# Windowed attention and two dense layers in float32: the first projections in five blocks of tokens (384, 512, 512, 512, 384) where there were six of 384, on one core

## The chip, the cores and the metric

The kernel runs on one core of one Trainium2 chip. The metric is the time of one execution in device microseconds (us), as a median of several runs. Profiles are of one execution each. TensorE (PE) multiplies matrices, VectorE (DVE), ScalarE (ACT) and GpSimd (POOL) work on tiles, SyncE (SP) issues loads.

## The reference

Everything is float32. Attention runs over 4 x 8 heads of 576 positions and 64 dimensions, and each position sees itself and the 63 before it. Its output, 2304 tokens of 512 numbers, goes through a gated product and two further layers:

```python
scores = scale * np.matmul(q, k.transpose(0, 1, 3, 2))
...
mask = (rel >= 0) & (rel < window)
scores = np.where(mask, scores, -1000000000.0)
...
attn = attn / (np.sum(attn, axis=-1, keepdims=True) + 1e-09)
return np.matmul(attn, v).astype(np.float32)
...
a = x @ w1
b = x @ w2
h = a * b @ w3
return (h @ w_out).astype(np.float32)
...
h = x @ w_in
g = h * (1.0 / (1.0 + np.exp(-h)))
return (g @ w_out).astype(np.float32)
```

w1 and w2 are 512 x 1024, w3 is 1024 x 1024, the first w_out 1024 x 512, w_in 512 x 2048 and the second w_out 2048 x 512.

## The kernel before, in words

**Stages.** The program has three stages, in this order.

1. `phase_w` multiplies w3 by the first w_out (matmul L482), so that the two layers become one matrix, `wp`. Weights arrive as 64-bit numbers and are converted on ACT, DVE and POOL. The first 14 groups of attention run between its matmuls.
2. `phase_a(blk, hooks)` is called once for each of six blocks of 384 tokens. It computes a = x w1, b = x w2, the product p = a b, and x2 = p wp, which goes to DRAM (`x2d`). Between its matmuls it runs the attention of the *next* block, and hooks of other work: in block 0 the rest of the conversions, in block 5 the conversion of the last two weights.
3. The last two layers run over blocks of 512 tokens (`emit_h`, L633, and `emit_o`, L652).

**Split operands.** A factor is held as a high part of reduced precision and the rest, and a product is three matmuls (`PASSES`). `split` makes the two parts: a copy on ACT (L79), a subtraction on POOL or DVE (L82).

**A block of `phase_a`.** It has 24 units. Units 0 to 15 are 12 matmuls each (L510) into one bank, `ab`, 8 pairs in turn: an even unit s gives a half of a, which ACT copies out (L516); the odd unit after it gives b, and DVE multiplies it by that copy (L518), after which ACT (L79) and POOL (L82) split the product into `p` or `q`. Units 16 to 23 are 12 matmuls each (L530), two units for each of four `x2` tiles, copied out by ACT (L535). So a block has 16 x 12 + 4 x 24 = 288 matmuls, each as wide as the block has tokens.

**A group of attention.** A group g is one unit of 128 tokens (`u`) and one pair of heads (`c`). There are 72, 12 for each block. A group is issued in two halves by `half(h)`, h = 2g and 2g + 1. The even half is: the scores of g on PE (L266, L270) and their mask and minimum on DVE (L276); the values of g-2 on PE (L343, L344); the transposes of g-1 on PE (L309), split by ACT (L319, L321) and DVE (L322, L324) into `pt`; the exponentials of g on ACT (L287). The odd half is: the sum's addition, the reciprocal and the product on DVE (L295, L297, L299), which finish `sm` of g; two copies on ACT (L349, L350), two additions on DVE (L351, L352) and one on POOL (L353), which put the values of g-2 into `xr`; the split of q and k of g+2 on ACT (L241), POOL (L245) and DVE (L248); the split of v of g. The first 17 groups (`plain`) are computed without split operands. They take other matmuls (L262, L336 to L338) and little on the other engines.

**What sets the order.** Every engine works through its instructions in the order in which the program issues them, and that order is written by hand: `unit(n)` issues one half in front of each unit (24 halves in 24 units), so that PE has one even half in front of every second unit. There is one bank for scores (`s`) and one for transposes (`t`). PE does the transposes of g-1 right after the scores of g, and they need `sm` of g-1 from DVE.

**Buffers.** Tiles of one tag share a buffer and wait for its last reader. Keys of plain groups (`k_p`) and the low part of keys of the others (`k_lo`) have buffers of their own, and so have the plain values `v_p` and the others.

Of the kernel before, what the change touches and what calls it, by code (L numbers as in the profile page):

```python
# [42 lines left out]
def tile_window_attention_ffn(ctx, tc, qkv, vp, mask, ident, w1, w2, w3t, w_out, w_in, w_out2, out):  # L43
# [158 lines left out]
    def plain(g):  # L202


        return g < PLAIN

    def place(g):
        blk, r = divmod(g, 3 * NPAIR)
        return blk * 3 + r % 3, r // 3

    def load_qk(g):
        if g < NG and g not in loaded:
            loaded.add(g)
            u, c = place(g)
# [4 lines left out]
            qk_raw[g] = att.tile([128, 128], F32, name=f"qp{g}", tag="qp", bufs=2)  # L219
            nc.sync.dma_start(out=qk_raw[g], in_=qkv[u, c, :, 0:128])  # L220

            for h, hs in HEADS:
                n = slice(384 + h * 192, 576 + h * 192)
                nc.sync.dma_start(out=k_p[g % 2][hs, h * 192 : h * 192 + 192], in_=qkv[u, c, hs, n])

    def load_v(g):
        if g < NG and ("v", g) not in loaded:
            loaded.add(("v", g))
            if plain(g):
                nc.sync.dma_start(out=v_p[g % 3], in_=vp[g])  # L230
                return
            v_raw[g] = att.tile([128, 3, 64], F32, name=f"v{g}", tag="v", bufs=3)
            u, c = place(g)
            nc.sync.dma_start(out=v_raw[g].rearrange("p t d -> p (t d)"), in_=qkv[u, c, :, 768:960])

    def prep_qk(g):
        if g >= NG or plain(g):
            return
        t = qk_raw.pop(g)
        hi = att.tile([128, 768], F32R, name=f"qkhi{g}", tag="qkhi", bufs=2)  # L240
        nc.scalar.copy(out=hi, in_=t)  # L241
        q, k = slice(128, 384), slice(384, 768)
        for h, hs in HEADS:
            n = slice(384 + h * 192, 576 + h * 192)
            nc.gpsimd.tensor_tensor(  # L245
                out=k_lo[g % 2][hs, h * 192 : h * 192 + 192], in0=t[hs, n], in1=f32(hi[hs, n]), op=ALU.subtract
            )
        nc.vector.tensor_tensor(out=hi[64:128, q], in0=t[64:128, q], in1=f32(hi[64:128, q]), op=ALU.subtract)  # L248
        qk_st[g] = hi

    def prep_v(g):
        if plain(g):
            return
        vhl = att.tile([128, 3, 2, 64], F32R, name=f"vhl{g}", tag="vhl", bufs=2)
        split(vhl[:, :, 0], vhl[:, :, 1], v_raw.pop(g), "act", "pool")
        v_st[g] = vhl

    def scores(g):
        s_ps = psa.tile([128, 2, 192], F32, name=f"s{g}", tag="s")
        t = qk_raw.pop(g) if plain(g) else qk_st.pop(g)  # L260
        if plain(g):
            nc.tensor.matmul(s_ps, lhsT=t[:, 0:128], rhs=k_p[g % 2], start=True, stop=True)  # L262
        else:
            for h in range(2):

                nc.tensor.matmul(  # L266
                    s_ps[:, h], lhsT=t[:, 128 + h * 128 : 256 + h * 128],
                    rhs=t[:, 384 + h * 192 : 576 + h * 192], start=(h == 0), stop=False,
                )
# [87 lines left out]
    def half(h):  # L357
# [4 lines left out]
        if not odd:  # L362
# [5 lines left out]
                split_t(g - 1, transposes(g - 1))  # L368
            if g < NG:
                exps(g)  # L370
            if g >= 2 and (g - 2) % (3 * NPAIR) == 3 * NPAIR - 1:
                sums.pop()()
        else:
            if g < NG:
# [21 lines left out]
            halves[0] += 1  # L396

    def split_x(blk, c):
        if c == 0:
            xhl[blk] = [slot(f"{t}{blk}", t, [2, 2, NB], F32R) for t in ("xa", "xb")]  # L400
        x = xhl[blk][c // 2][:, c % 2]
        split(x[:, 0], x[:, 1], xr[:, c], "act", "pool")


    W_HALVES = 28

    def phase_w():
        wo = slot("wo", "p", [8, 512])
        q = slot("q", "q", [2304])
# [80 lines left out]


    def phase_a(blk, hooks):
        x = xhl[blk]
        p = [slot(f"p{blk}", "p", [5, 2, NB], F32R), slot(f"q{blk}", "q", [3, 2, NB], F32R)]
        p = [p[f // 5][:, f % 5] for f in range(8)]
        a_sb = None

        def unit(n):
            halves_to(W_HALVES + 24 * blk + n + 1)
            hooks(n)  # L500

        for s in range(16):
            f, m = divmod(s, 2)
            unit(s)
            fs = slice((f % 4) * 128, (f % 4 + 1) * 128)
            acc = accumulator(f"ab{blk}_{s}", [128, NB])
            for k in range(4):
                w = weights["12", (2 * m + f // 4) * 4 + k]
                for n, (l, r) in enumerate(PASSES):
# [2 lines left out]
                        start=(k == 0 and n == 0), stop=(k == 3 and n == 2),  # L512
                    )
            if m == 0:
                a_sb = slot(f"a{blk}_{f}", "st", [2, NB], bufs=4)
                nc.scalar.copy(out=a_sb[:, 0], in_=acc)  # L516
            else:
                nc.vector.tensor_tensor(out=a_sb[:, 1], in0=acc, in1=a_sb[:, 0], op=ALU.mult)  # L518
                split(p[f][:, 0], p[f][:, 1], a_sb[:, 1], "act", "pool")
        for o in range(4):  # L520
            acc = accumulator(f"x2_{blk}_{o}", [128, NB])
            for f in range(8):
                if f % 4 == 0:
                    unit(16 + 2 * o + f // 4)
# [4 lines left out]
                for n, (l, r) in enumerate(PASSES):  # L529
# [178 lines left out]
def plain_values(qkv):  # L708
# [53 lines left out]
```

## Time and profile before

| | |
|---|---|
| median of 3 runs | 869.71 us (869.51 to 870.24) |
| the profiled execution | 868.85 us |
| its span, first to last instruction | 867.1 us |
| PE busy | 847.3 us (98%) |
| ACT busy | 497.8 us (57%) |
| DVE busy | 452.3 us (52%) |
| POOL busy | 445.6 us (51%) |
| `phase_w` | 9.6 to 97.6 us |
| block 0 of `phase_a` | 97.6 to 163.2 us |
| blocks 1 to 4, all with attention | 163.2 to 414.3 us |
| block 5 and the last two layers | from 414.3 us |

The shares of busy time are means over stages that differ: the engines other than PE do most of their work before 414.3 us. The profiled execution lies 0.86 us below the median and takes 1.75 us more than its span.

### The profile page before, as it was taken

Reading aid. Unit: us, or ns where it says so; the run is one execution under the profiler, and the core shown is the slowest. Engines: PE = TensorE matmul, PEld = TensorE weight load, DVE = VectorE, ACT = ScalarE, POOL = GpSimd, SP = SyncE. Lnnn points to the kernel's source line nnn. Section 1 sums busy time; section 2 is a strip of 40 time slices with the busy share of each in tenths; the row PEclk is TensorE's granted clock in tenths of the full one; section 3 lists DMA queues with packets and bytes.
Section 4 is the critical chain, followed back from the end, with each engine's and each line's share of the span. In section 5 each row is a group of like instructions: output and inputs, shape, how many; then the busy total and the mean of one; then the engine's idle time right before and its main releaser. Section 6 shows DMA issues by size and latency. Waiting matters only on the chain.

```text
span 867.1 us, 13353 instructions
## 1 busy us (share of the span) xinstructions
PE 847.3 (98%) x4362; PEld 737.0 (85%) x4362; DVE 452.3 (52%) x1158; ACT 497.8 (57%) x1243; POOL 445.6 (51%) x494
## 2 busy tenths in 40 slices
PE   5999999999999999999999999999999999999998
PEld 2444799999999999999998888888888888888896
DVE  5989878778778778676465884111111111111111
ACT  6888868788788788786666774222222222222222
POOL 4768566666666666665685886223322232223222
PEclk9999999999999999999999999999999999999999
DMA  8998233323333333330687200200020002000100
GB/s 296 336 291 261 95 97 108 120 92 101 120 92 110 112 95 120 118 92 33 245 319 274 82 1 0 98 1 1 0 98 1 1 0 73 2 1 0 49 1 25
DMA packets 43204, 85.83 MB, mean 99 GB/s; under 512 B 4864, under 2 KB 22528, under 8 KB 43136
## 3 DMA queue, kind: packets, MB, share of 16 engines
q1 hardware_dynamic: 37088, 75.55, 26.8%
q10 hardware_dynamic: 6048, 9.44, 3.0%
q8 instruction: 35, 0.57, 0.3%
q14 instruction: 33, 0.27, 0.1%
HBM read 75.53 MB, written 9.44 MB: 98 GB/s over the span
## 4 chain that ended last, share of the span: by engine, by line
PE 86%; DVE 1%; ACT 1%; issue 0%; POOLq 0%; POOL 0%; ACTq 0%; DVEq 0%
PE h L633 23%; PE o L652 23%; PE ab L510 22%; PE x L530 12%; PE t L309 2%; PE o L343 2%; PE s L266 1%; PE s L270 1%; PE o L344 1%; ACT sm L287 0%; DVE rs L295 0%; DVE a L518 0%; ACT p L79 0%; DVE cv_b L128 0%; POOLq L758 0%
## 5 line engine op out<-in xcount | busy, mean ns | idle before, releaser
L82 POOL TENSOR_TENSOR g<-sg,g 128x512 fp32r<-128x512 f32 (+1 forms) x80 | 94.9, 1186 | 249.6 <-ACT g L79 235.1
L633 PE MATMUL h<-x2t,hl 128*128 128x512 f32 (+1 forms) x960 | 213.4, 371 | 0.0
L652 PE MATMUL o<-hl,g 128*128 128x512 f32 x864 | 211.2, 391 | 0.1
L639 DVE TENSOR_TENSOR sg<-h,sg 128x512 f32<-128x512 f32 (+1 forms) x80 | 51.1, 638 | 288.2 <-ACT sg L638 288.2
L633 PEld LDWEIGHTS h<-x2t,hl 128*128 128x128 f32 x960 | 169.4, 188 | 33.9
L652 PEld LDWEIGHTS o<-hl,g 128*128 128x128 f32 x864 | 160.9, 188 | 35.6 <-POOL g L82 0.5
L638 ACT ACTIVATE sg<-h 128x512 f32<-128x512 f32 (+1 forms) x80 | 44.4, 555 | 195.4 <-PE h L633 195.4
L510 PE MATMUL ab<-xa,hl 128*128 128x384 f32 x576 | 119.2, 341 | 0.0
L510 PE MATMUL ab<-xb,hl 128*128 128x384 f32 x576 | 115.4, 334 | 0.0
L510 PEld LDWEIGHTS ab<-xb,hl 128*128 128x128 f32 x576 | 101.3, 188 | 0.0
L510 PEld LDWEIGHTS ab<-xa,hl 128*128 128x128 f32 x576 | 99.2, 188 | 0.0
L132 POOL TENSOR_TENSOR cv_b<-cv_b,cv_r 128x512 int32<-128x512 int32 x48 | 73.5, 1531 | 20.9 <-DVE cv_b L128 10.0
L79 ACT CAST g<-sg 128x512 fp32r<-128x512 f32 (+1 forms) x80 | 46.3, 578 | 63.2 <-DVE sg L639 62.3
L353 POOL TENSOR_TENSOR xr<-ot 128x128 f32<-128x128 f32 x55 | 31.5, 573 | 97.6 <-DVE ot L352 61.4
L245 POOL TENSOR_TENSOR klo<-qk,qkhi 64x192 fp32r<-64x192 f32 x110 | 66.7, 607 | 8.3 <-PE ab L510 2.0
L530 PE MATMUL x<-p,wp 128*128 128x384 f32 x360 | 68.2, 340 | 0.0
L287 ACT ACTIVATE sm<-sm,nm 128x192 f32<-128x192 f32 x144 | 64.4, 449 | 4.4 <-DVE nm L276 3.1
L530 PEld LDWEIGHTS x<-p,wp 128*128 128x128 f32 x360 | 61.9, 188 | 0.1
L125 DVE TENSOR_SCALAR cv_z<-cv_b 128x512 int32<-128x512 int32 x72 | 49.4, 687 | 15.5 <-ACT cv_b L114 14.6
L114 ACT ACTIVATE cv_b<-words 128x512 f32<-128x512 f32 x72 | 48.2, 670 | 9.7 <-DMA words<-in_w_out 5.2
L128 DVE SCALAR_TENSOR_TENSOR cv_b<-words,cv_z 128x512 int32<-128x512 int32 x72 | 49.4, 686 | 3.2
L115 ACT ACTIVATE cv_r<-words 128x512 int32<-128x512 uint32 x72 | 47.6, 661 | 0.0
(80 smaller groups left out, 1254.6 us busy)
## 6 DMA issues: line engine op xcount, KB each, us to landing
qk<-in_qkv SPq DMA_DIRECT2D x55, 384.0 KB, 3.2
words<-in_w_out SPq DMA_DIRECT2D x24, 512.0 KB, 8.3
words<-in_w3t SPq DMA_DIRECT2D x16, 512.0 KB, 6.0
words<-in_w SPq DMA_DIRECT2D x16, 512.0 KB, 6.4
words<-in_w_in SPq DMA_DIRECT2D x16, 512.0 KB, 7.2
v<-in_qkv SPq DMA_DIRECT2D x55, 96.0 KB, 2.7
x2d<-x2s ACTq DMA_DIRECT2D x24, 192.0 KB, 1.9
out_x<-osb ACTq DMA_DIRECT2D x18, 256.0 KB, 2.1
```

The lines of the kernel that those rows point to most:

```text
L82: (nc.vector if eng_lo == "dve" else nc.gpsimd).tensor_tensor(out=lo, in0=src, in1=f32(hi), op=ALU.subtract)
L114: nc.scalar.activation(out=f32(self.b), in_=f32(self.high), func=AF.Copy, scale=2.0**-112)
L125: nc.vector.tensor_scalar(out=self.z, in0=b, scalar1=3, scalar2=None, op0=ALU.logical_shift_left)
L128: nc.vector.scalar_tensor_tensor(out=b, in0=self.high, scalar=-0x80000000, in1=self.z, op0=ALU.bitwise_and, op1=ALU.bitwise_or)
L132: nc.gpsimd.tensor_tensor(out=x, in0=b, in1=self.r, op=ALU.add)
L245: nc.gpsimd.tensor_tensor(out=k_lo[g % 2][hs, h * 192 : h * 192 + 192], in0=t[hs, n], in1=f32(hi[hs, n]), op=ALU.subtract)
L287: nc.scalar.activation(out=x, in_=x, func=AF.Exp, scale=-1.0, bias=nm[:, h : h + 1], accum_out=rs[:, h : h + 1])
L510: nc.tensor.matmul(acc, lhsT=w[:, l, fs], rhs=x[k // 2][:, k % 2, r, :], start=(k == 0 and n == 0), stop=(k == 3 and n == 2),)
L530: nc.tensor.matmul(acc, lhsT=wp[f][:, l, o * 128 : (o + 1) * 128], rhs=p[f][:, r, :], start=(f == 0 and n == 0), stop=(f == 7 and n == 2),)
L633: nc.tensor.matmul(acc, lhsT=weights["in", f // 4, k][:, l, fs], rhs=x[:, k, r, :], start=(k == 0 and i == 0), stop=(k == 3 and i == 2),)
L639: nc.vector.tensor_tensor(out=sg, in0=acc, in1=sg, op=ALU.mult)
L652: nc.tensor.matmul(oacc[t], lhsT=g[:, l, t * 128 : (t + 1) * 128], rhs=weights["out", f][:, r, :], start=(f == 0 and i == 0), stop=(f == 1 ...
```

## The change: what it does

`UNITS = (3, 4, 4, 4, 3)` gives the tokens of a block, in units of 128: five blocks of 384, 512, 512, 512 and 384. Every tile and matmul of a block is as wide as its tokens. `place(g)` maps a group to its block by the same table, so blocks 1 to 3 have 16 groups each. In `unit(n)` the halves are spread by a rounded share: the 32 halves of a next block of 512 over 24 units, in a pattern of two, one, one. The slots for `p`, `q`, `xa`, `xb` and `xr` grow by a third. `k_p` and `k_lo` share one tag, `qp` shares that of `qkhi`, and both kinds of values share `v`; the zeros beside `k_lo` are written when it is first made. The addition of 1e-9 to the sums (L295) becomes a reduction over a pair, whose second element holds 1e-9.

```diff
-NB = 384
-NBLK = T // NB
 NU = T // 128
+UNITS = (3, 4, 4, 4, 3)
+NBLK = len(UNITS)
+FIRST = [sum(UNITS[:b]) for b in range(NBLK + 1)]
+NBM = max(UNITS) * 128
...
+def place(g):
+    b = max(n for n in range(NBLK) if FIRST[n] * NPAIR <= g)
+    c, r = divmod(g - FIRST[b] * NPAIR, UNITS[b])
+    return b, FIRST[b] + r, c
...
-    k_lo = [att.tile([128, 384], F32R, name=f"klo{i}", tag=f"klo{i}", bufs=1) for i in range(2)]
-    k_p = [att.tile([128, 384], F32, name=f"kp{i}", tag=f"kp{i}", bufs=1) for i in range(2)]
-    v_p = [att.tile([128, 320], F32, name=f"vp{i}", tag=f"vp{i}", bufs=1) for i in range(3)]
+    k_p = [att.tile([128, 384], F32, name=f"kp{i}", tag=f"k{i}", bufs=1) for i in range(2)]
+    k_lo = {}
+    sums_of = [att.tile([128, 2, 2], F32, name=f"es{i}", tag=f"es{i}", bufs=1) for i in range(2)]
+    for t in sums_of:
+        nc.vector.memset(t, 1.0e-9)
...
-        nc.vector.tensor_scalar_add(rs, rs, 1.0e-9)
+        nc.vector.tensor_reduce(out=rs, in_=sums_of[g % 2], axis=mybir.AxisListType.X, op=ALU.add)
...
-        x = xhl[blk]
-        p = [slot(f"p{blk}", "p", [5, 2, NB], F32R), slot(f"q{blk}", "q", [3, 2, NB], F32R)]
+        x, nb = xhl[blk], UNITS[blk] * 128
+        ahead = 2 * NPAIR * UNITS[blk + 1] if blk + 1 < NBLK else 0
+        begun = W_HALVES + 2 * NPAIR * (FIRST[blk + 1] - UNITS[0])
+        p = [slot(f"p{blk}", "p", [5, 2, nb], F32R), slot(f"q{blk}", "q", [3, 2, nb], F32R)]
...
         def unit(n):
-            halves_to(W_HALVES + 24 * blk + n + 1)
+            halves_to(begun + -(-ahead * (n + 1) // 24) if ahead else LAST_HALF)
             hooks(n)
```

Two places show what moves. The first is PE in block 0, units 10 to 13 before. `s` are scores, `o` values, `t` transposes, `ab` a unit's matmuls; 24 matmuls stand between one group's transposes and the next group's scores:

```order
L309 MATMUL t_1436<-id_sb,sm_73 128x128 x3
L510 MATMUL ab_12_1448<-xa_414,hl 128x384 x6
L510 MATMUL ab_12_1448<-xb_415,hl 128x384 x6
L510 MATMUL ab_13_1484<-xa_414,hl 128x384 x6
L510 MATMUL ab_13_1484<-xb_415,hl 128x384 x6
L266 MATMUL s_1500<-qkhi_1396 128x192 x2
L270 MATMUL s_1500<-klo_75,qkhi_1396 128x384
```

The same engine and block of the changed kernel, units 12 to 14:

```order
L326 MATMUL t_1544<-id_sb,sm_73 128x128 x3
L529 MATMUL ab_12_1577<-xa_415,hl 128x384 x6
L529 MATMUL ab_12_1577<-xb_416,hl 128x384 x6
L283 MATMUL s_1592<-qkhi_1504 128x192 x2
L287 MATMUL s_1592<-klo_1093,qkhi_1504 128x384
L360 MATMUL o_1600<-pt_982,vhl_1509 128x256 x2
L361 MATMUL o_1600<-pt_979,vhl_1509 128x4x64
L326 MATMUL t_1604<-id_sb,sm_72 128x128 x3
L529 MATMUL ab_13_1616<-xa_415,hl 128x384 x6
L529 MATMUL ab_13_1616<-xb_416,hl 128x384 x6
L529 MATMUL ab_14_1653<-xa_415,hl 128x384 x6
L529 MATMUL ab_14_1653<-xb_416,hl 128x384 x6
```

The distance between groups was 24 matmuls throughout; now it is 12 and 24 in turn, in blocks 0, 1 and 2. The second place is ACT at the same point of block 0, before; one turn of a group from its casts of `pt` on:

```order
L319 CAST pt_972<-t_1436 128x2x128
L321 CAST pt_970<-t_1436 64x64 x2
L287 ACTIVATE sm_72,rs_1429<-sm_72,nm_1428 128x192 x2
L516 COPY a_6_1461<-ab_12_1448 128x384
L349 COPY ot_1466<-o_1432 64x256
L350 COPY ot_1466<-o_1432 64x256
L241 CAST qkhi_1472<-qk_1324 128x768
L79 CAST vhl_1477<-v_1328 128x3x64
L79 CAST q_978<-a_6_1461 128x384
```

And the changed kernel, from the cast of `q` that stands in front of the group with the short distance:

```order
L90 CAST q_988<-a_5_1493 128x384
L336 CAST pt_982<-t_1544 128x2x128
L338 CAST pt_980<-t_1544 64x64 x2
L304 ACTIVATE sm_72,es_76<-sm_72,nm_1536 128x192 x2
L366 COPY ot_1559<-o_1540 64x256
L367 COPY ot_1559<-o_1540 64x256
L257 CAST qkhi_1565<-qk_1436 128x768
L90 CAST vhl_1570<-v_1378 128x3x64
L535 COPY a_6_1590<-ab_12_1577 128x384
L336 CAST pt_981<-t_1604 128x2x128
L338 CAST pt_979<-t_1604 64x64 x2
L304 ACTIVATE sm_73,es_77<-sm_73,nm_1596 128x192 x2
```

In each turn before there stood one copy of `a` and one cast of a product beside the group's own work; now three pairs of them go with four groups.

## Rows read from the trace of the kernel before

**Rows 1.** Windows (`phase_w`, blocks 0, 1, 4): length, busy PE, PEld, DVE, ACT, POOL, granted clock.

```profile
9.60:97.60 88.00, 80.86 (x277) 42.83 (x277) 76.33 (x175) 71.53 (x173) 60.67 (x48) 1.00 0.85 275
97.60:163.20 65.60, 64.92 (x409) 64.28 (x407) 50.95 (x151) 51.00 (x149) 42.55 (x54) 1.00 0.34 106
163.20:226.50 63.30, 63.30 (x400) 63.14 (x398) 49.01 (x164) 51.92 (x157) 40.22 (x61) 1.00 0.34 107
353.10:414.30 61.20, 61.20 (x381) 61.04 (x380) 43.42 (x144) 46.52 (x141) 35.45 (x54) 1.00 0.24 73
```

**Rows 2.** Waits of PE over the span: us in total, times, longest.

```profile
PE t L309 <- DVE sm L299: 3.0, 3, 1.6
```

**Rows 3.** Timeline of PE, three stretches: start us, us, engine, line, operation, count.

```profile
98.72 1.21 PE L510 MATMUL ab<-xb,hl 128*128 128x384 f32 x6
...
100.81 0.85 PE L510 MATMUL ab<-xb,hl 128*128 128x384 f32 x4
...
599.95 2.88 PE L633 MATMUL h<-x2t,hl 128*128 128x512 f32 x12
602.67 2.88 PE L652 MATMUL o<-hl,g 128*128 128x512 f32 x12
...
500.37 2.98 PE L633 MATMUL h<-x2t,hl 128*128 128x512 f32 x12
503.18 2.01 PE L652 MATMUL o<-hl,g 128*128 128x512 f32 x8
```

**Rows 4.** Timeline of one group's turn in block 1, all engines.

```profile
203.47 0.48 ACT L516 COPY a<-ab 128x384 f32<-128x384 f32 x1
203.48 0.43 DVE L295 TENSOR_SCALAR rs<-rs 128x2 f32<-128x2 f32 x1 [0.22 <-ACT sm L287]
...
204.14 0.56 DVE L299 TENSOR_TENSOR sm<-sm,rs 128x384 f32<-128x384 f32 x1
204.34 0.36 PE L266 MATMUL s<-qkhi 128*128 128x192 f32 x2
...
204.73 0.83 ACT L241 CAST qkhi<-qk 128x768 fp32r<-128x768 f32 x1
...
205.09 0.49 PE L309 MATMUL t<-id_sb,sm 128*128 128x128 f32 x3
205.24 0.43 DVE L352 TENSOR_TENSOR ot<-o,ot 64x256 f32<-64x256 f32 x1
205.34 2.87 PE L530 MATMUL x<-p,wp 128*128 128x384 f32 x15
...
205.60 0.42 DVE L248 TENSOR_TENSOR qkhi<-qk,qkhi 64x256 fp32r<-64x256 f32 x1
...
206.06 0.56 DVE L518 TENSOR_TENSOR a<-ab,a 128x384 f32<-128x384 f32 x1
...
206.53 0.35 DVE L276 CUSTOM_DVE_ANT_0 sm<-s,mask_sb 128x192 f32<-128x192 f32 x1
206.65 0.51 ACT L79 CAST q<-a 128x384 fp32r<-128x384 f32 x1 [0.83 <-DVE a L518]
...
207.07 0.37 ACT L319 CAST pt<-t 128x256 fp32r<-128x256 f32 x1
...
207.79 0.46 ACT L287 ACTIVATE sm<-sm,nm 128x192 f32<-128x192 f32 x1
207.80 0.42 DVE L322 TENSOR_TENSOR pt<-t,pt 128x256 fp32r<-128x256 f32 x1 [0.63 <-ACT pt L321]
...
208.20 1.02 POOL L82 TENSOR_TENSOR q<-a,q 128x384 fp32r<-128x384 f32 x1
...
208.81 0.43 DVE L295 TENSOR_SCALAR rs<-rs 128x2 f32<-128x2 f32 x1 [0.23 <-ACT sm L287]
```

**Rows 5.** One line's instructions, L295: shortest, median, longest ns.

```profile
L295 DVE TENSOR_SCALAR rs<-rs x72: 152/432/1140, 13.8 to 402.7; 128x2 f32<-128x2 f32 x72
```

**Rows 6.** Groups by line and shape: busy us, mean ns of one.

```profile
L639 DVE TENSOR_TENSOR sg<-h,sg 128x512 f32<-128x512 f32 x64 | 44.3, 692 | 250.3 <-ACT sg L638 250.3
```

More of the change, by code (lines that the diff above doesn't have):

```diff
@@ L64, in tile_window_attention_ffn @@
     x2d = dram.tile([4, 128, T], F32, name="x2d", tag="x2d")
-    SLOTS = {"p": 4096, "q": 2304, "xa": 1536, "xb": 1536, "xr": 1536, "st": 1024, "x2": 4096, "cv_r": 512, "cv_b": 512}
+    SLOTS = {
+        "p": 10 * NBM, "q": 6 * NBM, "xa": 4 * NBM, "xb": 4 * NBM, "xr": 4 * NBM,
+        "st": 1024, "x2": 4096, "cv_r": 512, "cv_b": 512,
+    }
     def slot(name, tag, dims, dtype=F32, pool=None, bufs=1):
@@ L213, in load_qk @@
             loaded.add(g)
-            u, c = place(g)
+            _, u, c = place(g)
             if not plain(g):
@@ L218, in load_qk @@
                 return
-            qk_raw[g] = att.tile([128, 128], F32, name=f"qp{g}", tag="qp", bufs=2)
+            qk_raw[g] = att.tile([128, 768], F32, name=f"qp{g}", tag="qkhi", bufs=2)[:, 0:128]
             nc.sync.dma_start(out=qk_raw[g], in_=qkv[u, c, :, 0:128])
@@ L228, in load_v, with zero_beside @@
             loaded.add(("v", g))
+            v_raw[g] = att.tile([128, 320], F32, name=f"v{g}", tag="v", bufs=3)
             if plain(g):
-                nc.sync.dma_start(out=v_p[g % 3], in_=vp[g])
+                nc.sync.dma_start(out=v_raw[g], in_=vp[g])
                 return
-            v_raw[g] = att.tile([128, 3, 64], F32, name=f"v{g}", tag="v", bufs=3)
-            u, c = place(g)
-            nc.sync.dma_start(out=v_raw[g].rearrange("p t d -> p (t d)"), in_=qkv[u, c, :, 768:960])
+            _, u, c = place(g)
+            nc.sync.dma_start(out=v_raw[g][:, 0:192], in_=qkv[u, c, :, 768:960])
+    def zero_beside(t):
+        for h, hs in HEADS:
+            nc.gpsimd.memset(t[hs, 192 - h * 192 : 384 - h * 192], 0.0)
     def prep_qk(g):
@@ L239, in prep_qk @@
         t = qk_raw.pop(g)
+        if g % 2 not in k_lo:
+            k_lo[g % 2] = att.tile([128, 384], F32R, name=f"klo{g % 2}", tag=f"k{g % 2}", bufs=1)
+            zero_beside(f32(k_lo[g % 2]))
         hi = att.tile([128, 768], F32R, name=f"qkhi{g}", tag="qkhi", bufs=2)
@@ L254, in prep_v @@
         vhl = att.tile([128, 3, 2, 64], F32R, name=f"vhl{g}", tag="vhl", bufs=2)
-        split(vhl[:, :, 0], vhl[:, :, 1], v_raw.pop(g), "act", "pool")
+        v = v_raw.pop(g)[:, 0:192].rearrange("p (t d) -> p t d", t=3)
+        split(vhl[:, :, 0], vhl[:, :, 1], v, "act", "pool")
         v_st[g] = vhl
@@ L276, in scores @@
             nc.vector.tensor_tensor_reduce(
-                out=sm[g % 2][:, h, :], in0=s_ps[:, h, :], in1=mask_sb[:, mask_kind(place(g)[0]), 64 - 64 * h : 256 - 64 * h],
+                out=sm[g % 2][:, h, :], in0=s_ps[:, h, :], in1=mask_sb[:, mask_kind(place(g)[1]), 64 - 64 * h : 256 - 64 * h],
                 op0=ALU.add, op1=ALU.min, scale=-(D ** -0.5), scalar=3.0e38, accum_out=nm[:, h : h + 1],
@@ L287, in exps @@
             nc.scalar.activation(
-                out=x, in_=x, func=AF.Exp, scale=-1.0, bias=nm[:, h : h + 1], accum_out=rs[:, h : h + 1]
+                out=x, in_=x, func=AF.Exp, scale=-1.0, bias=nm[:, h : h + 1], accum_out=sums_of[g % 2][:, h, 0:1]
             )
@@ L326, in values @@
     def values(g):
-        u, c = place(g)
-        r = u % 3 * 128
+        b, u, c = place(g)
+        r = (u - FIRST[b]) * 128
         tag = "z" if done["step"] == len(line) and g % 2 else "o"
@@ L370, in half @@
                 exps(g)
-            if g >= 2 and (g - 2) % (3 * NPAIR) == 3 * NPAIR - 1:
+            if g >= 2 and (g - 1) // NPAIR in FIRST[1:] and (g - 1) % NPAIR == 0:
                 sums.pop()()
@@ L398, in split_x @@
     def split_x(blk, c):
+        nb = UNITS[blk] * 128
         if c == 0:
-            xhl[blk] = [slot(f"{t}{blk}", t, [2, 2, NB], F32R) for t in ("xa", "xb")]
+            xhl[blk] = [slot(f"{t}{blk}", t, [2, 2, nb], F32R) for t in ("xa", "xb")]
         x = xhl[blk][c // 2][:, c % 2]
-        split(x[:, 0], x[:, 1], xr[:, c], "act", "pool")
+        split(x[:, 0], x[:, 1], xr[:, c, 0:nb], "act", "pool")
     W_HALVES = 28
@@ L408, in phase_w @@
         wo = slot("wo", "p", [8, 512])
-        q = slot("q", "q", [2304])
+        q = slot("q", "q", [2048])
         for i in range(2):
@@ L444, in phase_w @@
         ready += [W12_B + 24 + (4 if W12_B == 16 else 0)] * 2
-        for t in k_p + [f32(t) for t in k_lo]:
-            for h, hs in HEADS:
-                nc.gpsimd.memset(t[hs, 192 - h * 192 : 384 - h * 192], 0.0)
+        for t in k_p:
+            zero_beside(t)
         loads_to(2)
@@ L505, in phase_a @@
             fs = slice((f % 4) * 128, (f % 4 + 1) * 128)
-            acc = accumulator(f"ab{blk}_{s}", [128, NB])
+            acc = accumulator(f"ab{blk}_{s}", [128, nb])
             for k in range(4):
@@ L520, in phase_a @@
         for o in range(4):
-            acc = accumulator(f"x2_{blk}_{o}", [128, NB])
+            acc = accumulator(f"x2_{blk}_{o}", [128, nb])
             for f in range(8):
@@ L533, in phase_a @@
                     )
-            x2 = slot(f"x2s{blk}_{o}", "st", [NB], bufs=4)
+            x2 = slot(f"x2s{blk}_{o}", "st", [nb], bufs=4)
             nc.scalar.copy(out=x2, in_=acc)
-            nc.scalar.dma_start(out=x2d[o, :, blk * NB : (blk + 1) * NB], in_=x2)
+            nc.scalar.dma_start(out=x2d[o, :, FIRST[blk] * 128 : FIRST[blk + 1] * 128], in_=x2)
     def new_pt():
@@ L548, in tile_window_attention_ffn @@
     with tc.manual_schedule():
-        xr = slot("xr", "xr", [4, NB])
+        xr = slot("xr", "xr", [4, NBM])
         phase_w()
@@ L712, in plain_values @@
     for g in range(PLAIN):
-        blk, r = divmod(g, 3 * NPAIR)
-        x = qkv[blk * 3 + r % 3, r // 3, :, 768:960]
+        _, u, c = place(g)
+        x = qkv[u, c, :, 768:960]
         v[g, :, 0:64], v[g, :, 128:192] = x[:, 0:64], x[:, 64:128]
```

7 lines of the change are left out of this document (2 added, 5 removed).

## The prediction

> **What bounds the kernel now.** I read the windows by stage first, because a share over the whole span mixes stages. In block 1 PE is busy for all of its 63.30 us, and so it is in block 4; block 0 lacks 0.7 us and `phase_w` 7 us [rows 1]. So PE bounds `phase_a`, and its time falls only if PE gets less to do. The clock needs no term: the granted share is 1.00, the 2.4 GHz level, in every stage, `phase_w` with its pauses among them.
>
> The next view is the timeline of PE, which tells what a matmul costs. Twelve of 384 columns take from 98.72 to 100.81 less six, that is six per 1.04 and 173 ns each; twelve of 512 take 2.72 us, 227 ns each, around 600 us, and 2.81 us, 234 ns, around 500 us [rows 3]. From 384 to 512 columns the cheap spacing grows by 54 ns, which is 128 columns at 2.4 GHz; so about 13 ns of each matmul do not depend on its width. These 13 ns are what fewer and wider matmuls save.
>
> The third view is the timeline of one group's turn, because an engine that PE never waits for can still be close behind. L295 begins at 203.48 and again at 208.81: the chain through DVE and ACT takes 5.33 us for one group. It runs: sum, reciprocal, product (L299), two additions (0.43 each, the second ends at 205.67), subtraction L248, product L518, then on ACT the cast that waited 0.83 us for L518, the casts of `pt`, the exponentials, and the next L295 [rows 4]. PE's own turn is 24 x 0.1733 plus the group's matmuls. Those follow from block 1: 63.30 less 288 x 0.1733 = 49.9 leaves 13.4 for 12 groups, 1.11 each. That makes 5.27. So the chain is already slower than PE by 0.06 us a turn. L299 ends at 204.70 and the transposes that need it begin at 205.09 [rows 4], with 0.39 us left. PE hides the chain, but only just.
>
> **The change part by part.**
>
> *Fewer matmuls.* 6 x 288 = 1728 matmuls of 384 columns (299.5 us) become 576 of 384 (99.8 us) and 864 of 512 (195.9 us with 227 ns): -3.8 us. The other end, 234 ns, makes 202.2 and +2.5 us. I take 227: the stretch at 600 us multiplies tiles in slots of `main` alone (x2 of an odd block in `p`, weights in `w`), as `phase_a` does, while at 500 us x2 and weights lie in the pool `end`. One sentence beside it: the Trainium skill, page "TensorE: Matmul & The Clock Gate", section "Wait — 56ns, not 53.3ns?", gives 2.5 ns as the fixed part of a warm matmul, by which an estimate of the gain is 288 x 2.5 ns = 0.7 us and not 3.8, so that the page speaks against the change. The spacings of both widths contradict it here, and the sum goes by them.
>
> *The turns of block 0.* This is the large term. Block 0 stays 384 wide, but now carries 16 groups and not 12. The distance between groups is 12 and 24 matmuls in turn. In six units PE needs 72 x 0.1733 + 4 x 1.11 = 16.9 us for four groups. I follow the chain for these four, with the durations of [rows 4]:
> - First turn, whose odd half comes at once behind the even half. On DVE: reduction and reciprocal 0.40 (0.66 from L295 to L299, with 0.17 for 0.43, see below), L299 0.59, additions 0.89, subtraction 0.45, product L518 0.59, gaps of 0.03 included. On ACT: cast 0.42, `pt` 0.72, exponentials 1.02. Together 5.1.
> - Second turn: a copy of `a` (0.48) stands ahead on ACT, and the way leads over the copies of `ot` and the cast of `qkhi`, as in the turn shown: 5.3.
> - Third and fourth turn: no product between subtraction and mask. Third, on DVE: 0.40 + 0.59 + 0.89 + 0.45, the mask operation (L276, two at 0.35), exponentials 1.02, and a product ahead of the reduction 0.59: 4.6. Fourth, ACT without a pause: cast 0.51, copies of `ot` 0.78, `qkhi` 0.83, v 0.25, copy of `a` 0.48, `pt` 0.72, exponentials 1.02: 4.6.
>
> That is 19.6 against 16.9: PE, with one bank of transposes, stands still for 2.7 us in six units, most of it at the second short distance, where `sm` comes some 2 us late. Units 5 to 15 hold 11/6 of this, 4.9 us. Units 0 to 4 have plain groups, which ask little of DVE and ACT, but the last conversions too: 1 us, between 0 and 2. In units 16 to 23 no products stand in the chain, but the copies of `x2` and the splits of `xa` do: at the short distances 1.4 and 0.3 us late, 1.7. Sum +7.6. Bounds: if only throughput counted, ACT has 51.0 us now and about 3.3 more for each of four groups (51.92 [rows 1] less some 12 for the block's own 24 copies and casts at about 0.5, over 12), 64 against PE's 69, and the term is nearly 0. If the reduction is no faster than L295, it is 16 x 0.26 = 4 us more, 12.
>
> *Blocks 1 and 2*, 512 wide with 16 groups: six units last 72 x 0.2267 + 4 x 1.11 = 20.8 on PE, and the chain, with products of 0.69 for 0.56 [rows 6], about 20.1. On average it fits. One short distance in four does not: from a group's first score to the transposes that need it PE takes 1.11 + 12 x 0.2267 + 0.75 = 4.58 (0.75 from scores to transposes, 204.34 to 205.09 [rows 4]), and where a product and its cast come first, `sm` is ready at 4.9. Twice in each block: +1.4 with what the reduction's end adds; 0 to 3. Block 3 has 24 halves, one ahead of each unit, and PE's turn is 6.6 against 5.2: no wait.
>
> *The reduction.* No row shows one. L295 takes 0.15 at least and 0.43 as its median [rows 5]; in the turn shown it ends at 209.24, when POOL's subtraction of 208.20 ends (209.22). So L295 is short, but waits for POOL's instruction. I take 0.17 for a reduction, the short kind, and 0.43 as the other end. A sentence beside it: the Trainium skill, page "SBUF — State Buffer", section "Who interferes with whom", says that a reduction never contends for the port pair that DVE and GpSimd share, which the row cannot show for this operation. In `phase_w` L295 waits up to 1.14 us, but L299 behind it reads two tiles, and has to wait for the same POOL instruction if the first does not: -0.3, at most -2.3, what PE waited there for `sm` (3.0 in all [rows 2] less the 0.7 of block 0). Those 0.7 of block 0 are in the 1 us of its first units, so they come off once: -0.7.
>
> *At nothing:* shared buffers (the reader before is two groups back, and SP issues its loads in the same order), the four zero fills moved to POOL in block 0, two fills of `sums_of` on DVE ahead of all work, longer and fewer copies, stores of `x2`. They lie on engines with at least 11 us free in a block [rows 1], and in block 4 and the last two layers no instruction moves.
>
> **Sum.** -3.8 + 7.6 + 1.4 - 0.3 - 0.7 = +4.2. The profiled execution took 868.85, so 873.0; the median lies 0.86 above it: **873.9 us**.
>
> **The rivals.**
> - *The chain is hidden.* If ACT and DVE work off the short distances without holding up PE, the terms of blocks 0 to 2 are about 1: 869.7 - 3.8 - 0.3 - 0.7 + 1 = 865.9. For it: both engines are busy for 82% or less of block 1. Against it: ACT stood waiting for L518 in the turn shown, and the chain is at 5.33 there. It decides for faster below 3.1 us of waits in blocks 0 to 2.
> - *The two cancel*, waits of 3 to 6.5 us: about 869.7.
> - *Slow reduction* (0.43): 16 groups in block 0 and the short distances in 1 and 2: +5, 879.
> - *Wide matmuls at 234 ns*: +6.3, 880. Against it: the slots are those of the cheap stretch.
>
> **Chances.** Forecast (871.5 to 877) 0.57, slow reduction 0.08, wide spacing 0.05, cancelled 0.13, hidden 0.17. Within 0.2% (868.0 to 871.4) is about what a measurement of this kernel cannot tell from no change. So slower 0.70, same 0.13, faster 0.17. The range from 867.5 to 879.5 leaves out most of the hidden case and the far end of the wide one.
>
> **What would show it.** In the changed profile: L529's spacing at 227 ns in blocks 1 to 3; block 0 at some 76 us and not 65.6, with PE waiting for L316 at every second or fourth transpose and longest about 2 us; blocks 1 and 2 at 83.1 + 0.7; block 3 at 76.6 without waits; the reduction near 0.17 us. Wrong would be a block 0 of 70 us, or waits of PE on loads.

## The result, and the profile after

The changed kernel takes 876.77 us (median of 4 runs, 876.75 to 877.43) against 869.65: 1.0082 times as long, with a 95% interval of 1.0068 to 1.0095. It is slower by 7.1 us, where +4.2 was forecast. The profiled execution took 877.43, the longest of the four, and its mean granted clock is 0.997 where the others have 0.999 to 1.000; so its profile shows some 0.7 us more than the median.

The page of the changed kernel, span and busy time:

```profile
span 875.3 us, 12769 instructions
PE 849.7 (97%) x4074; PEld 700.4 (80%) x4074; DVE 435.6 (50%) x1152; ACT 491.4 (56%) x1219; POOL 443.6 (51%) x482
```

PE has 288 instructions less, and its idle time has grown. The windows by stage say where (length, then busy PE, PEld, DVE, ACT and POOL, granted clock, DMA share, GB/s): blocks 0 to 3, then the last two layers.

```profile
97.20:177.70 80.50, 74.12 (x445) 70.33 (x444) 62.17 (x203) 64.24 (x193) 53.42 (x74) 0.98 0.35 111
177.70:262.00 84.30, 83.84 (x436) 71.47 (x434) 61.06 (x217) 67.37 (x202) 53.60 (x77) 1.00 0.33 106
262.00:345.80 83.80, 83.62 (x435) 71.39 (x433) 61.07 (x217) 66.85 (x201) 53.00 (x77) 1.00 0.34 108
345.80:422.40 76.60, 76.60 (x381) 64.91 (x379) 42.40 (x144) 48.62 (x140) 38.29 (x55) 1.00 0.20 66
468.20:871.40 403.20, 403.08 (x1850) 333.27 (x1848) 105.56 (x152) 136.72 (x248) 147.03 (x117) 1.00 0.09 32
```

Read them against [rows 1]. The first projections begin at 97.20 us, 0.4 earlier than before. Blocks 0 to 3 hold all of the attention that blocks 0 to 4 held. They take 325.2 us (97.2 to 422.4) where the old five took 316.7 (97.6 to 414.3), that is 8.5 more; the last block and the last two layers are unchanged. Block 3, with one half ahead of each unit, has no idle time at all and the length that was forecast (76.6). Blocks 1 and 2 are 1.2 and 0.7 us longer than PE's own 83.1. Block 0 is 80.5 us long; PE's own work there is about 69.3 (64.9 in block 0 before, and 1.11 for each of four more groups). So the loss lies in block 0.

Who PE waits for there (us in total, times, longest):

```profile
PE t L326 <- DVE sm L316: 3.5, 4, 1.1
PE t L326 <- ACT qkhi L257: 0.8, 1, 0.8
PE o L353 <- ACT xr L356: 0.6, 1, 0.6
PE s L283 <- DVE nm L293: 0.5, 1, 0.5
PE o L360 <- DVE pt L339: 0.4, 1, 0.4
PE o L360 <- POOL vhl L93: 0.3, 1, 0.3
```

The largest is the one that [rows 2] showed before with 3.0 us in the whole span: transposes that need `sm`. One of these in the timeline, at the second short distance of six units:

```profile
142.15 0.47 PE L360 MATMUL o<-pt,vhl 128*128 128x256 f32 x2 [0.30 <-POOL vhl L93]
142.59 0.16 DVE L312 TENSOR_REDUCE rs<-es 128x2 f32<-128x4 f32 x1 [0.23 <-ACT sm L304]
142.78 0.17 DVE L314 RECIPROCAL rs<-rs 128x2 f32<-128x2 f32 x1
142.98 0.56 DVE L316 TENSOR_TENSOR sm<-sm,rs 128x384 f32<-128x384 f32 x1
143.69 0.52 PE L326 MATMUL t<-id_sb,sm 128*128 128x128 f32 x3 [0.82 <-DVE sm L316]
```

DVE was not slow: it waited for the exponentials on ACT, ran reduction, reciprocal and product in a row, and PE went on 0.15 us after the product. The chain simply began too late. The next view is the clock around 123 us, in three windows:

```profile
115.70:123.10 7.40, 5.08 (x31) 4.06 (x30) 5.93 (x17) 5.63 (x17) 5.46 (x7) 1.00 0.22 66
123.20:126.50 3.30, 3.30 (x12) 3.30 (x13) 2.18 (x8) 2.11 (x9) 1.74 (x3) 0.50 0.29 74
126.60:130.00 3.40, 3.40 (x23) 3.40 (x23) 2.21 (x7) 2.03 (x5) 1.11 (x1) 1.00 0.38 122
```

PE was busy for 5.08 of 7.40 us, its waits adding up to 2.3, and then ran at 0.50, the 1.2 GHz level, for 3.4 us: 12 matmuls and transposes where the next stretch of that length has 23. That costs some 1.6 us here, which nothing in the profile before had shown. It is no constant of the kernel: by their mean clocks (0.999, 1.000 and 1.000) the other three executions can have had a part of it at most, and they are only 0.6 to 0.7 us shorter.

### The profile page after: what moved, and what is told of

It reads as the page before. It is cut to its first block, busy times and chain, and to the rows that moved or that the text cites. A ratio compares the mean times of both kernels' runs of the same rounds, so it can differ in the third digit from the quotient of the medians.

```text
span 875.3 us, 12769 instructions
## 1 busy us (share of the span) xinstructions
PE 849.7 (97%) x4074; PEld 700.4 (80%) x4074; DVE 435.6 (50%) x1152; ACT 491.4 (56%) x1219; POOL 443.6 (51%) x482
## 4 chain that ended last, share of the span: by engine, by line
PE 78%; ACT 5%; DVE 2%; issue 2%; POOL 1%; DMA 0%; ACTq 0%; POOLq 0%; DVEq 0%
PE h L652 23%; PE o L671 22%; PE ab L529 19%; PE x L549 8%; PE t L326 2%; ACT sm L304 1%; PE o L360 1%; ACT qkhi L257 1%; PE s L283 1%; PE s L287 1%; PE o L361 1%; ACT pt L338 1%; ACT pt L336 0%; ACT ot L367 0%; DMA qk<-in_qkv 0%
## 5 line engine op out<-in xcount | busy, mean ns | idle before, releaser
L93 POOL TENSOR_TENSOR g<-sg,g 128x512 fp32r<-128x512 f32 (+1 forms) x80 | 94.8, 1184 | 249.7 <-ACT g L90 235.1
L652 PE MATMUL h<-x2t,hl 128*128 128x512 f32 (+1 forms) x960 | 213.4, 371 | 0.0
L671 PE MATMUL o<-hl,g 128*128 128x512 f32 x864 | 211.2, 391 | 0.1
L652 PEld LDWEIGHTS h<-x2t,hl 128*128 128x128 f32 x960 | 169.4, 188 | 33.9
L671 PEld LDWEIGHTS o<-hl,g 128*128 128x128 f32 x864 | 160.9, 188 | 35.6 <-POOL g L93 0.5
L529 PE MATMUL ab<-xa,hl 128*128 128x512 f32 (+1 forms) x480 | 116.9, 379 | 0.0
L529 PE MATMUL ab<-xb,hl 128*128 128x512 f32 (+1 forms) x480 | 112.4, 369 | 0.0
L529 PEld LDWEIGHTS ab<-xb,hl 128*128 128x128 f32 x480 | 88.4, 189 | 11.7
L529 PEld LDWEIGHTS ab<-xa,hl 128*128 128x128 f32 x480 | 85.8, 190 | 9.6
L143 POOL TENSOR_TENSOR cv_b<-cv_b,cv_r 128x512 int32<-128x512 int32 x48 | 73.5, 1532 | 20.6 <-DVE cv_b L139 13.5
L549 PE MATMUL x<-p,wp 128*128 128x512 f32 (+1 forms) x300 | 67.8, 374 | 0.0
L549 PEld LDWEIGHTS x<-p,wp 128*128 128x128 f32 x300 | 53.5, 188 | 6.4
L293 DVE CUSTOM_DVE_ANT_0 sm<-s,mask_sb 128x192 f32<-128x192 f32 x144 | 45.4, 353 | 4.5 <-PE s L287 3.0
```

Of the source, the lines that this page charges most:

```text
L93: (nc.vector if eng_lo == "dve" else nc.gpsimd).tensor_tensor(out=lo, in0=src, in1=f32(hi), op=ALU.subtract)
L143: nc.gpsimd.tensor_tensor(out=x, in0=b, in1=self.r, op=ALU.add)
L529: nc.tensor.matmul(acc, lhsT=w[:, l, fs], rhs=x[k // 2][:, k % 2, r, :], start=(k == 0 and n == 0), stop=(k == 3 and n == 2),)
L549: nc.tensor.matmul(acc, lhsT=wp[f][:, l, o * 128 : (o + 1) * 128], rhs=p[f][:, r, :], start=(f == 0 and n == 0), stop=(f == 7 and n == 2),)
L652: nc.tensor.matmul(acc, lhsT=weights["in", f // 4, k][:, l, fs], rhs=x[:, k, r, :], start=(k == 0 and i == 0), stop=(k == 3 and i == 2),)
L671: nc.tensor.matmul(oacc[t], lhsT=g[:, l, t * 128 : (t + 1) * 128], rhs=weights["out", f][:, r, :], start=(f == 0 and i == 0), stop=(f == 1 ...
```

## The experiments

My theory: block 0 carries 16 groups of attention beside matmuls of 384 columns, and the chain through DVE and ACT is too long for that. Rivals: the shared buffers, the reduction, the short distances by themselves, or the first units of block 0 with their conversions and the change from plain groups.

**1. Six blocks, all else as changed** (`e1_six_blocks`). The slot of `p` keeps its old size; in the changed kernel it is a quarter larger, and the other four slots are a third larger.

```diff
-UNITS = (3, 4, 4, 4, 3)
+UNITS = (3, 3, 3, 3, 3, 3)
```

> Six blocks of 384 again, but with the shared buffers and the reduction. Theory (block 0 has too much attention for its width, nothing else in the change costs): no wait of PE in blocks 1 to 4, block 0 at 65 to 66 us, median 869.0 to 869.8. Rival (the shared buffers or the reduction cost time): 872 or more, with new waits of PE on loads, on POOL or on DVE in blocks that are as wide as before.

868.88 us, ratio 0.9986 (0.9975 to 0.9996). Blocks 0 and 1:

```profile
100.30:165.40 65.10, 64.78 (x410) 64.14 (x408) 48.00 (x152) 51.17 (x149) 43.51 (x58) 1.00 0.34 107
165.40:228.80 63.40, 63.20 (x398) 62.88 (x397) 46.46 (x164) 52.06 (x157) 39.93 (x61) 1.00 0.35 107
```

This profile is of an execution of 871.74 us: in its first stage PE waited 2.37 us for a load and then ran at half clock (mean 0.83 from 30 to 40 us), so block 0 begins 3 us later. The blocks themselves are as long as before. So the shared buffers and the reduction cost nothing and give a little; the widths and what goes with them make the loss.

**2. The addition in place of the reduction** (`e2_addition`).

```diff
-accum_out=sums_of[g % 2][:, h, 0:1]
+accum_out=rs[:, h : h + 1]
...
-        nc.vector.tensor_reduce(out=rs, in_=sums_of[g % 2], axis=mybir.AxisListType.X, op=ALU.add)
+        nc.vector.tensor_scalar_add(rs, rs, 1.0e-9)
```

> The changed kernel with the addition of 1e-9 as it was (L295's form) in place of the reduction. Theory (the addition waits for POOL, and in a chain that PE waits for this shows): 0.1 to 0.26 us more in each of the 16 turns of block 0, so block 0 at 82 to 84 us and a median of 878 to 881. Rival (the wait for POOL only moves on to the product behind it): 876.5 to 877.5, unchanged.

883.64 us, ratio 1.016 (1.0141 to 1.018), and more than I had expected (878 to 881). The windows of blocks 0 to 2:

```profile
97.60:181.40 83.80, 76.07 (x446) 71.92 (x444) 65.07 (x204) 64.49 (x193) 53.46 (x74) 0.96 0.35 107
181.40:266.60 85.20, 84.10 (x434) 71.37 (x433) 63.51 (x216) 67.47 (x202) 53.47 (x77) 1.00 0.34 105
266.60:351.50 84.90, 84.06 (x436) 71.45 (x434) 63.49 (x216) 67.16 (x202) 53.04 (x77) 1.00 0.34 106
```

Block 0 has the 82 to 84 us that the theory gave, but in part by another way: it is 3.3 us longer than in the changed kernel, and some 1.6 of that is a second fall of the clock, at 160 to 170 us (mean 0.83). All five executions have a mean clock of 0.994 to 0.998, so the 6.9 us between the medians hold the addition and the falls that came with it. Blocks 1 and 2, at 1.00, are 1 us longer each. A few tenths of a microsecond in the chain reach PE. In blocks of 384 with 12 groups the same exchange, with the shared buffers, is worth the 1.2 us of experiment 1.

**3. Even distances** (`e3_even_spread`). The halves are issued in steps of three matmuls, so that 18 matmuls stand between any two groups of blocks 0 to 2. The last `split_x` of a block moves from f = 0 to f = 2.

```diff
+        def step(n):
+            halves_to(begun + -(-ahead * (n + 1) // 96) if ahead else LAST_HALF)
...
             for k in range(4):
+                if k:
+                    step(4 * s + k)
...
+                if f % 4:
+                    step(4 * (16 + 2 * o) + f)
+                if blk + 1 < NBLK and o == 3 and f == 2:
+                    split_x(blk + 1, 3)
```

> The changed kernel with the halves spread over 96 steps of 3 matmuls, not over 24 units of 12: in blocks 0 to 2 every distance between groups is 18 matmuls, none is 12. Theory (block 0 has more work for DVE and ACT than its PE time covers, however it is spread): block 0 stays at 75 us or more, blocks 1 and 2 fall to 83.1 us, median 872 to 876. Rival (it is the short distances, not the amount): block 0 at 69 to 71 us, median 865 to 868.

873.29 us, ratio 1.0031 (1.0023 to 1.004), within the theory's forecast. Blocks 0 and 1:

```profile
97.30:175.30 78.00, 71.52 (x443) 68.50 (x442) 63.37 (x203) 64.04 (x193) 55.21 (x74) 1.00 0.38 115
175.30:258.60 83.30, 83.30 (x434) 71.41 (x433) 61.20 (x216) 67.56 (x201) 53.62 (x77) 1.00 0.35 107
```

Block 1 has no wait left, and the clock does not fall in this execution, but block 0 stays 8.7 us above PE's 69.3. In the wide blocks it was the short distance, in block 0 it is the amount, though some 2 us of the 8.7 are lost before 118 us, around the change from plain groups, and 1.7 behind the last group (see 11).

**4. Four groups moved to the first stage** (`e4_groups_to_w`).

```diff
-    W_HALVES = 28
+    W_HALVES = 36
...
-        begun = W_HALVES + 2 * NPAIR * (FIRST[blk + 1] - UNITS[0])
+        begun = 28 + 2 * NPAIR * (FIRST[blk + 1] - UNITS[0])
+        if blk == 0:
+            begun, ahead = W_HALVES, begun + ahead - W_HALVES
```

> The changed kernel with four groups of attention more in the first stage (36 halves ahead of block 0 and not 28), so that block 0 has 12 groups at even distances, as before the change. Theory (the amount in block 0): block 0 at 63 to 66 us, the first stage 6.4 to 9 us longer (four plain groups at 1.6 us and some waits), blocks 1 and 2 as in the changed kernel, no fall of the clock, median 868 to 871. Rival (the waits in block 0 come from the last conversions and the change from plain groups, not from the amount): block 0 keeps 5 us of waits or more, median 873 or more.

882.15 us, ratio 1.0131 (1.0115 to 1.0148): a miss. The windows are the first stage, the first units of block 0 and the rest of it.

```profile
16.00:109.60 93.60, 85.56 (x319) 47.08 (x318) 74.90 (x192) 74.56 (x190) 64.08 (x57) 1.00 0.80 258
109.60:127.00 17.40, 12.20 (x67) 11.58 (x68) 16.25 (x37) 13.67 (x36) 10.32 (x13) 0.93 0.21 65
127.00:181.90 54.90, 54.54 (x329) 54.22 (x329) 41.85 (x139) 44.07 (x131) 37.84 (x53) 0.96 0.33 102
```

The first stage ends 12.4 us later than in the changed kernel and not 6.4 to 9: it had no room either. In the first units of block 0 PE stands idle for 5 us, most of it for one wait on the additions of `ot` (4.2 us), and the clock falls for 6.8 us. Block 0 takes 72.3 us, and its waits and the median are those given for the rival: it is right about those units in this version. Behind them, with 12 groups at even distances, PE is busy for 54.54 of 54.90 us, as the theory wants, though the first 4.4 of these at half clock.

**5. The pool of the last layers, 32 bytes moved** (`e5_end_pool_at_64`). This tests the choice between 227 and 234 ns for a wide matmul.

```diff
-        "st": 1024, "x2": 4096, "cv_r": 512, "cv_b": 512,
+        "st": 1024, "x2": 4104, "cv_r": 512, "cv_b": 512,
```

> The changed kernel, with 32 bytes more in the slot of x2 of the pool for the last layers, so that x2 of even blocks and the first five weights of the last layers begin at multiples of 64 bytes, as the slots of the other pool do, and not 32 bytes behind one. Theory (matmuls at 234 ns and not 227 are those whose operands lie 32 bytes off, so the choice of 227 for the first projections was one of addresses): no stretch of the last layers at 232 to 234 ns, some 950 matmuls of 512 columns at 5 ns less each, median 871.5 to 872.5. Rival (it is the pool, or a neighbour that works at the same time): 876.5 to 877.5, spacings unchanged.

875.36 us, ratio 1.0066 (1.0052 to 1.008), 1.4 less than the changed kernel where 4.3 to 5.3 less was expected. The timeline of PE where the slow spacing was:

```profile
507.78 2.93 PE L652 MATMUL h<-x2t,hl 128*128 128x512 f32 x12
510.54 2.93 PE L671 MATMUL o<-hl,g 128*128 128x512 f32 x12
513.31 0.87 PE L652 MATMUL h<-x2t,hl 128*128 128x512 f32 x3
```

Twelve take 2.76 us, 230 ns each, between the 227 and 234 of [rows 3]. In the changed kernel the two lines differed in this stretch:

```profile
505.78 2.92 PE L671 MATMUL o<-hl,g 128*128 128x512 f32 x12
508.54 2.98 PE L652 MATMUL h<-x2t,hl 128*128 128x512 f32 x12
511.36 2.92 PE L671 MATMUL o<-hl,g 128*128 128x512 f32 x12
```

L652 took 2.82 us for twelve and L671 2.76 already; only L652 became faster. The last two layers take 401.5 us (467.9 to 869.4) where they took 403.2, that is 1.7 less. The offset is a part of it; what makes the rest stays open.

**6. The subtraction of q on POOL** (`e6_subtract_on_pool`).

```diff
-        nc.vector.tensor_tensor(out=hi[64:128, q], in0=t[64:128, q], in1=f32(hi[64:128, q]), op=ALU.subtract)
+        nc.gpsimd.tensor_tensor(out=hi[64:128, q], in0=t[64:128, q], in1=f32(hi[64:128, q]), op=ALU.subtract)
```

> The changed kernel with the subtraction for the low part of q (64x256, 0.42 us on DVE) on POOL. Theory (the chain over DVE and ACT holds PE up in block 0): three of four turns are 0.45 us shorter, the waits of block 0 from unit 6 on fall by about 3 us, block 0 at 75 to 78 us, median 871 to 875. Rival (POOL or the first units' conversions set the pace of block 0): block 0 at 80 us or more, median 876 or more.

880.57 us, ratio 1.0127 (1.0114 to 1.0141): a miss. Block 0, at 80.2 us, and the median are where the rival put them; block 1 takes 85.8. DVE's chain is 0.42 us shorter on paper, and in block 0 PE's waits for `sm` did fall, from 3.5 to 1.9 us (1.0 by name, and 0.9 that the profile puts down to `vhl`, see below). A new wait came in their place, for the moved subtraction itself (total, times, longest):

```profile
PE s L283 <- POOL qkhi L264: 3.0, 3, 1.5
```

The timeline at the same short distance shows a second effect:

```profile
142.07 0.16 DVE L312 TENSOR_REDUCE rs<-es 128x2 f32<-128x4 f32 x1 [0.22 <-ACT sm L304]
142.35 1.01 POOL L93 TENSOR_TENSOR q<-a,q 128x384 fp32r<-128x384 f32 x1
142.46 1.31 DVE L316 TENSOR_TENSOR sm<-sm,rs 128x384 f32<-128x384 f32 x1
143.80 0.42 DVE L368 TENSOR_TENSOR ot<-o,ot 64x256 f32<-64x256 f32 x1
143.91 0.52 PE L326 MATMUL t<-id_sb,sm 128*128 128x128 f32 x3 [0.86 <-ACT vhl L90]
```

The product takes 1.31 us and not 0.56 while POOL's subtraction of `q` (L93) runs, which has moved back behind the added one. The line says "vhl", but that is not what PE waited for, as the product ended at 143.77. The wait came back in other places, so this shows that POOL has no room for the subtraction; it neither confirms nor refutes the theory of the changed kernel.

**7. The step up in width one block later** (`e7_blocks_33444`).

```diff
-UNITS = (3, 4, 4, 4, 3)
+UNITS = (3, 3, 4, 4, 4)
```

> Blocks of 384, 384, 512, 512 and 512 tokens: now block 0 has 12 groups and block 1, 384 wide and without conversions or plain groups, has 16. Theory (16 groups are too much for a block of 384, wherever it stands): block 0 at 64.5 to 65.5 us, block 1 at 74 to 77 us, median 870.5 to 875. Rival (the waits are those of the first units, with conversions and the change from plain groups): block 1 at 68 to 70 us, without waits, median 864.5 to 867.

874.42 us, ratio 1.0058 (1.0046 to 1.0071). Blocks 0 and 1, both 384 wide:

```profile
97.60:162.60 65.00, 64.72 (x409) 64.08 (x407) 47.93 (x151) 51.07 (x149) 43.53 (x58) 1.00 0.35 107
162.60:238.60 76.00, 70.87 (x434) 67.59 (x432) 60.09 (x216) 64.16 (x201) 50.36 (x77) 1.00 0.38 115
```

The waits have moved with the 16 groups: 76.0 us for block 1, whose matmuls and groups take 67.7 (288 x 0.1733 + 16 x 1.11), and block 0, with all the conversions and the change from plain groups, is at 65.0. This is the run that separates the theory from the first-units rival, and the rival falls as the main cause.

**8. Even distances and the subtraction on POOL** (`e8_even_and_pool`), the edits of 3 and 6 together.

> Even distances of 18 matmuls and the subtraction on POOL together. Theory (the chain's length per group is what binds, and distances and length add up): block 0 at 73 to 76 us, blocks 1 and 2 at 83.2, median 867.5 to 871.5. Rival (one of the two takes away all that there is to gain): no better than the better of the two alone.

874.3 us, ratio 1.0062 (1.0048 to 1.0075), no better than 3 alone, as the rival had it; block 0 at 79.2. The subtraction on POOL gives nothing, as in 6.

**9 and 10. More plain groups** (`e9_even_21_plain`, `e10_even_25_plain`), on top of 3.

```diff
-PLAIN = 17
+PLAIN = 21
```

> Even distances as in the even spread, and 21 plain groups in place of 17. A plain group takes about 0.5 us more of PE (1.6 and not 1.1) and about half of ACT's and DVE's time. Theory (in block 0 ACT and DVE are about 9 us behind PE's work): four groups give back 4 x 2.3 us of it and cost 4 x 0.5 us of PE, block 0 at 71 to 74 us, median 866 to 870. Rival (the waits of block 0 hang on the conversions and on the change from plain groups, wherever that falls): block 0 at 78 us or more, median 873 or more.

> The same with 25 plain groups. Theory: PE's own work in block 0 is then 69.3 + 8 x 0.5 = 73.3 us and binds, so block 0 is at 73.5 to 76 us and the median 1 to 3 us above that with 21: 868 to 872. Rival (ACT and DVE are still behind, or plain groups cost PE nothing where it waits): faster than with 21.

870.32 us (1.0009, 0.9994 to 1.0024) and 871.28 us (1.0021, 1.0009 to 1.0034), the first just above its forecast; the two intervals overlap. Block 0 with 21:

```profile
97.30:172.10 74.80, 71.88 (x453) 69.33 (x451) 54.07 (x179) 56.92 (x173) 45.46 (x58) 1.00 0.39 111
```

Four groups with more matmuls and less of everything else shorten block 0 by 3.2 us against run 3, and eight lengthen it again, to 76.2, in the one profile of each. That the block gets shorter when PE is given more to do is what a chain over the other engines predicts; the rival said 78 us or more. A plain group asks less of POOL too, so these runs do not say how the chain divides among ACT, DVE and POOL.

**11 and 12. The best of either width** (`e11_wide_mended`: 9 with the bytes of 5 and the last `split_x` at f = 5; `e12_six_and_64`: 1 with the bytes of 5).

> Blocks of 384, 512, 512, 512, 384 with even distances, 21 plain groups, 32 bytes more in the slot of x2 of the last pool, and the last split of the next block's x three matmul groups later (f = 5 and not 2), so that ACT does not stand behind POOL's xr while PE wants transposes. Theory (the waits left in block 0 of the version with 21 plain groups are that one, 1.9 us, and the moved bytes give 1.1 to 1.4 us): block 0 at 73 us, median 866.5 to 868.5. Rival (a later split only moves the wait to the next block's first matmuls): block 0 at 74.5 to 75.5 us, median 868.5 to 869.5.

> Six blocks of 384 with the reduction and the shared buffers, and 32 bytes more in the slot of x2 of the last pool. Theory (no block carries more attention than its width covers, so only the small gains show): 1.1 to 1.4 us under the same without the bytes, median 867 to 868. Rival (the bytes' gain was a chance of addresses in one version): 868.5 to 869.5.

The wide one takes 869.73 us (1.0003, 0.9995 to 1.0012), nearest to its rival: block 0 stays at 74.9 and its last transposes still wait 1.72 us, so the place of the split was not the cause. The timeline of DVE shows what stands ahead of them:

```profile
169.33 0.42 DVE L368 TENSOR_TENSOR ot<-o,ot 64x256 f32<-64x256 f32 x1 [0.93 <-ACT ot L367]
169.76 0.43 DVE L369 TENSOR_TENSOR ot<-o,ot 64x256 f32<-64x256 f32 x1
170.22 0.16 DVE L312 TENSOR_REDUCE rs<-es 128x2 f32<-128x4 f32 x1
```

At a block's last group `half` issues the two additions of `ot` ahead of the reduction (everywhere else behind it), so the reduction waits for ACT's copies of `ot`, though its exponentials ended at 168.59. The changed kernel has the same order there; no run altered it.

The narrow one takes 865.87 us, 0.9958 (0.9944 to 0.9971), below both forecasts, and is faster than the kernel before and the changed one. Its last two layers:

```profile
459.30:860.80 401.50, 401.35 (x1849) 332.90 (x1847) 105.51 (x152) 136.72 (x248) 146.84 (x117) 1.00 0.09 32
```

They are 1.7 us shorter than in the changed kernel (403.2), as in 5 and in the wide one (401.5 in each). The remaining 1.7 of the 3.4 us under the kernel before are near the 1.2 of experiment 1; what the last half microsecond is, these runs don't show.

## Why the prediction was right, point by point

The time came out 2.9 us above the forecast of 873.9 and only 0.2 us inside the upper end of its range of 871.5 to 877: the mechanism was the one that was forecast, but that the range held is in part luck.

- **Fewer matmuls, -3.8 us: right.** Block 3 came out at the 76.6 us that 288 x 227 ns and the 11.3 us of its groups give. The Trainium skill's 2.5 ns for the fixed part of a matmul (page "TensorE: Matmul & The Clock Gate", section "Wait — 56ns, not 53.3ns?") does not agree with these matmuls: with it block 3 would be near 73.5 us, an estimate from 288 x 10.8 ns less.
- **The turns of block 0: the mechanism right, the size 3.6 us short** (80.5 against 76.9). Read from PE's starts, against the same stretch without a wait, units 0 to 4 lost 1.2 us (1 forecast); units 5 to 15 lost 5.5 (4.9), most of it at the second short distance as forecast, 2.5 and 1.9; units 16 to 23 lost 2.3 (1.7), at their short distances 1.4 and 0.4 (1.4 and 0.3). Another 0.9 was lost at the group ahead of block 1's first unit, for which the sum had no term (the order told in 11). That makes 9.9 for 7.6. The rest of block 0, some 1.6 us, is the clock, and here a step failed in the profiled execution: "the clock needs no term". Waits of 2.3 us within 7.4 were followed by 3.4 us at 1.2 GHz. With these figures the sum is -3.8 + 9.9 + 1.9 - 0.4 - 0.7 = 6.9, near the 7.1 between the medians, and 8.5 with the clock, near the 8.6 between the profiled executions; so what the median lacked was mostly the waits. That the amount binds is shown by runs 3, 7 and 9; that the short distances matter in the wide blocks, by run 3.
- **Blocks 1 and 2, +1.4 us: near in sum (1.9), wrong in place.** I had put two waits into each block, at short distances where a product and its cast come first. They came at the first short distance of both blocks (0.8 and 0.4 us); the later ones lost 0.1 at most, so the turn there was shorter than I worked out. The copies of `x2` and the splits of `xa` and `xb`, which stand ahead of the first units on ACT, may be the cause; no run tried that.
- **The reduction: right.** It took 144 to 159 ns in all 72 cases, beside POOL or not, where L295 took up to 1140 [rows 5]. In this the trace agrees with the Trainium skill, page "SBUF — State Buffer", section "Who interferes with whom". Run 2 shows what it is worth here: 6.9 us, falls of the clock among them, more than the 5 of that rival.
- **The first stage, -0.3 us: right** (0.4).
- **The rival of a hidden chain** fell with block 0; that of wide matmuls at 234 ns with block 3.

The line for the reduction in the changed kernel (shortest, median, longest ns):

```profile
L312 DVE TENSOR_REDUCE rs<-es x72: 144/157/159, 14.1 to 406.9; 128x2 f32<-128x4 f32 x72
```

## What to carry to other kernels

Where work for the next block runs under the matmuls of this one, a wider next block puts more of it under the same matmuls. So compare the length of the chain through the other engines with PE's turn before you widen, not their busy shares: at 82% ACT had already no room here. Wider matmuls saved 3.8 us in all; the one step up in width cost 8 to 11, in whichever block it stood. And a piece taken off one engine in such a chain is only a gain if the engine that gets it has room at that point and does not slow down the one that lost it (run 6).

## What the runs showed of the hardware

- Short pauses of PE in quick succession (5.08 us busy of 7.40) were followed by 3.4 us at half clock in one execution of the changed kernel; two of the others have a mean clock of 1.000. The same number of groups at even distances kept 1.00 in block 0 of run 3's profile. In run 1's profile a single wait of 2.37 us in the first stage was followed by half clock too.
- A DVE product of two SBUF tiles took 1.31 us and not 0.56 beside a POOL subtraction of 1.01, while the reduction ahead of it took its usual 0.16.
- Matmuls of 512 columns took 227, 230 or 234 ns with operands in other places. An offset of 32 bytes is a part of the reason (2.82 to 2.76 us for twelve of one line, and 1.7 us in the last two layers of runs 5, 11 and 12); the rest was not found.
